# Batch 0's q through TensorE, low parts of w_spatial moved, and a new written order in a memory-attention and spatial-gate kernel

## The chip, the cores and the metric

One NeuronCore of a Trainium2 chip runs the whole program. Its engines work in parallel, each through its own queue in order: TensorE (PE; its weight loads are PEld), VectorE (DVE), ScalarE (ACT), GpSimd (POOL), and SyncE (SP), which issues all the loads and stores. The metric is the device time of one execution in microseconds. The kernel before was timed three times: median 435.25 us, from 434.84 to 436.11.

## The reference

Two stages over 8 batches, 8 heads, 576 positions, head size 64 and 32 memory slots. The first is an attention over memories that are weighted means of k and v:

```
a = softmax(phi over the 32 slots)                 # (b, h, s, m)
k_m, v_m = a^T k, a^T v                            # (b, h, m, d)
attn = softmax(q k_m^T / 8);  x = attn v_m         # heads side by side: (b, s, 512)
```

The second is a gated layer with a mixing over the positions:

```
h = relu(x @ w_in);  u, v = h[..., :512], h[..., 512:]
v_n = (v - mean(v)) / sqrt(var(v) + 1e-6)
v_s = w_spatial @ v_n + b_spatial[:, None]         # over the 576 positions
out = (u * v_s) @ w_out
```

w_in is 512 x 1024, w_spatial 576 x 576, w_out 512 x 512. w_in and w_out arrive as float64 and the other inputs as float32.

## The kernel before

Every large product is made from parts. A matrix is cut into a high part that TensorE takes at its fast rate and a low part, the rest (`hi`, `lo`; in names `h` and `l`), and three products, high by high, high by low and low by high, add up in PSUM. The low part is made in one of two ways by `low` (lines 152 to 163): VectorE subtracts the high part from the value in PSUM, or TensorE adds minus the high part to that PSUM tile (the matrix `minus`, line 157) and ScalarE copies the rest out. The set `ON_VECTOR` (line 50) says by name which way is taken, and in the same manner which engine does the additions and multiplications of the decoding.

w_in and w_out are decoded on the chip from the two 32-bit words of each float64 (`decode`, lines 177 to 223): VectorE takes the exponent (`power`) and the mantissa, ScalarE converts, and VectorE or GpSimd adds and multiplies. w_in comes in eight pieces of 128 rows and 512 columns; pairs of pieces are decoded together, E0 and E1 for the v half of w_in, L0 and L1 for the u half.

For each batch there are nine kinds of work, each a Python generator that yields between steps: P (softmax weights of phi), K (loads k and v, makes the memories: `kvm`, then the transposes `tk` and `tv`, then `kT` and `vT`), Q (loads q and transposes it into `qT`), S (scores `sc`, softmax `sm`, then `aT` and its parts `ah` and `al`), M (products `mp` of v_m with w_in, parts `mh` and `ml`), U (`pu`, the u half), V (`pv`, the v half with its normalization), G (`ps`, the mixing with w_spatial, times u, parts `gh` and `gl`), and O (`po`, the projection, and the store). Weights have their own kinds: D loads w_in, E and L decode it, X decodes w_out, W loads w_spatial, T transposes it (T0 to T3 by 128 columns, T4 the last 64; tiles `wt`, results `wth`, `wtl`, `ws1`, `ws2`), B sets the bias.

Nothing schedules this at run time. The string `START` (line 26) lists the steps of batch 0 and of all the weights, with the first steps of batches 1 and 2 (a prime is one batch ahead); `PLAN` (line 41) is the repeated list for batches 1 to 7. Each step issues its instructions at once, so these strings set the order in each engine's queue, that of SP's loads included. PSUM has four tiles of one bank (`bank`) and two of two banks (`banks`) that all the kinds share in turn: an instruction that writes a tile waits until the readers of its last use are done.

Batch 0's q is loaded in four transfers (lines 429 to 438), each of 32 partitions and runs of 32 floats, and VectorE transposes blocks of 32 by 32 (line 441).

Of the kernel before, what the change touches and what calls it, by code (L numbers as in the profile page):

```python
# [23 lines left out]


START = """
    D1 P W T3 P T3 B D0 T3 D0 T3 P*2 D1 T3 T2 L0 P E0 D1 T2*2 P T2 T3*2 P K P E0*2 L0 D1 P*2 K
    L0*2 E1 W P D0 L0 T2 P W D0 T1*2 E0 K T2 T1 E0 P W Q E1*2 L0 T1 E1 P L0 P E1 T1 E0*2 K T1 L1
    E0 Q K E1 P' L1 K L0 T2 L1 T1 E1 L1*2 K W E1 T4 K*2 L1 Q*3 K Q K'*2 P' K*2 P' T0 S P' S T0
    S*3 P' M1 P' S M1 T0 M1 P'*2 L1 P' M1 S P' S B M1 S L1 S P' T4*2 X1 T4*2 X0 T0 S M1 T0 M0 P'  # L30
    M1 P' S M0 K' T0 T4 M0 S M0 T0 T4 P' S M0 S*3 X0*2 S X0 P' S K' M0 X1 U0 X1*2 X0 U1 V1 M0 X0
    Q' V0 X1 X0 V1 X0 K'*2 V1 K' V0 X1*2 K' Q' U0 U1 X0 V3 U1 K' X1 U0 K' V1*2 U2 V2 V0 X1 V3*2
    V4 V1*2 X0 K'*2 V0 Q'*2 V0*3 V4 U3 U2 V2 Q' U3 X1 X0 Q' U2 V4 V3*2 U3 S' V2 S'*2 X1 S' V2 S'
    P'' X2 V2 X2 S' Q'' G0 X3 G1 M0' V3 V4 M1' V3 V2 V4*2 V2 P'' M1' X2 V4*2 K'' M0' G1 X2*2 M0'
    G0 P'' M1' G1 M1' P'' G0 P'' G1 G0 P'' M0' K'' G1 G3 X3 G0 S' G2 X2 P'' G1 G0 G3 X2 M1' G1
    X2 G0 M0' G2 M1' X3 G1 P'' G3 M0' P'' G2 G3 G0*2 G1 P'' G2 X2 M0' S' X3 G3 X3*2 X2 X3 O3 G2
    S' X3 O2 G2 G3 M1' G2 O1 X2 O0 X3*2 G3*2 G2 X3 G2 O3 S' P'' S' O1 S'*2 O3*2 P'' S' O1 O2 S'
    O0 S'*2 P'' O2 S'*2 P'' O1 G3 O2 P'' O0*2
"""

PLAN = """
    P'*4 K' U0 V1 V0 K' U0 V2 U0 K' U2 V0 V1 U1 V1 V0 V2 V1 V2 K' V0 V4 U1 V1 V3 Q' K' V0 P'' V1
    U1 K' U3 U2 V1 Q' V4 V2 V3 K' V2 V4 V3 K'*2 P''*4 U3 V4 K' S' U2 U3 V2 V3 V4 K'' S' V3 S'*2
    G0 V4 V3 G1 P'' S' M0'*2 Q'' P'' M1' G0 S' V2 S' M1' V4 G1 M1' V4 G0 V3 S' G1 Q G0 M1' M0'
    M1' P'' S' G1 G0 P'' M1' G2 S' G1 K'' G1 M0' S' G0 S' G1 G0*2 Q'' G3 G0 G2 S' G1 G3 G1 G2 G3
    G2 P'' S' G2*2 M1' G3*2 O3 G3 S'*2 O0 S' G2 G3 O1 O0 G3 P'' S' O0 S' O0 O1 O3 G3 Q'' O3 O4
    M0' G2 O3 O2 O1 V0' G2 O4 M0'*2 O1 O4 V0' Q'' O2 O4 O2*2
"""
# [9 lines left out]
def memory_attention_spatial_gate(  # L58
# [386 lines left out]
    def scores(b, _):  # L447
# [42 lines left out]
        state["a", b] = ah, al  # L490
        for r in range(2):
            for c in range(2):
                nc.vector.transpose(
                    aT[:, r].rearrange("p (i c x) -> p c i x", c=2, x=32)[:, c], sm[:, r, c]
                )
# [6 lines left out]
            yield
# [264 lines left out]
```

## Time and profile before

| | |
|---|---|
| median of 3 runs | 435.25 us |
| the profiled execution | 435.84 us |
| its span, first to last instruction | 434.1 us |
| TensorE busy | 400.4 us (92%) |
| VectorE busy | 294.9 us (68%) |
| ScalarE busy | 223.0 us (51%) |
| GpSimd busy | 74.0 us (17%) |
| mean granted TensorE clock | 0.971 |

The shares are means over the whole span, and the span has two unlike parts: the first 58 us, in which weights are loaded, decoded and transposed and the attention of batch 0 is made, and the rest. Line 634 (mixing) has 28% of the chain that ended last, line 674 (projection) 23%.

### The profile page before, as it was taken

The page shows a single profiled execution, that of the slowest core. Times are in us where ns is not written, and L with a number is a line of the kernel's source. Part 1 is how long each engine was busy: PE and PEld are TensorE (multiplying, and loading weights), DVE is VectorE, ACT ScalarE, POOL GpSimd, SP SyncE. Part 2 cuts the span into 40 slices and gives each one's busy share as a digit, 9 for nine tenths or more (in the row PEclk, how much of TensorE's full clock was granted, in tenths as well). Part 3 has the DMA queues.
Part 4 walks back from the last instruction along what each step waited for, and adds up shares of the span by engine and source line. Part 5 has one row for each costly group of instructions (what it writes and reads, how often), then busy time and mean ns, then how long its engine had stood idle before and what let it go on. Part 6 is the DMA issues. An engine that isn't in the chain of part 4 may idle for free.

```text
span 434.1 us, 9211 instructions
## 1 busy us (share of the span) xinstructions
PE 400.4 (92%) x3815; PEld 333.1 (77%) x3815; DVE 294.9 (68%) x546; ACT 223.0 (51%) x427; POOL 74.0 (17%) x148
## 2 busy tenths in 40 slices
PE   0436699999999999999999999999999999999996
PEld 0233297988889787988888887988798787988985
DVE  1599989995899338954898349954896358824420
ACT  1663578753854348343943368244833276337412
POOL 1007237240400032000400022002300030003000
PEclk9985689999999999999999999999999999999999
DMA  8999916807890169403980359214940300010003
GB/s 292 405 192 360 123 57 99 271 0 149 208 181 2 72 179 210 47 24 113 204 142 2 112 176 203 16 73 132 210 68 24 98 2 2 2 74 23 2 2 121
DMA packets 94543, 50.69 MB, mean 117 GB/s; under 512 B 75491, under 2 KB 79587, under 8 KB 94501
## 3 DMA queue, kind: packets, MB, share of 16 engines
q1 hardware_dynamic: 94500, 50.10, 47.5%
q8 instruction: 30, 0.49, 0.5%
q14 instruction: 13, 0.10, 0.1%
HBM read 40.65 MB, written 9.44 MB: 115 GB/s over the span
## 4 chain that ended last, share of the span: by engine, by line
PE 87%; DVE 6%; DMA 4%; ACT 1%; issue 1%; SPq 0%; DVEq 0%; ACTq 0%
PE ps L634 28%; PE po L674 23%; PE pv L547 13%; PE pu L596 12%; PE kvm L371 4%; PE mp L517 4%; DMA raw<-in_moe_w_in_dram 2%; DMA w_rem<-in_moe_w_spatial_dram 2%; PE sc L455 2%; DVE power L206 1%; DVE win_sb L214 1%; DVE win_sb L219 1%; DVE qT L441 1%; DVE half L317 0%; DVE g L645 0%
## 5 line engine op out<-in xcount | busy, mean ns | idle before, releaser
L634 PE MATMUL ps<-wth,vh 128*128 128x288 f32 x256 | 57.8, 307 | 0.1
L559 POOL TENSOR_SCALAR rs<-mv 128x1 f32<-128x1 f32 (+1 forms) x40 | 10.1, 253 | 262.7 <-DVE mv L556 238.0
L634 PE MATMUL ps<-wth,vl 128*128 128x288 f32 x256 | 54.6, 295 | 0.0
L634 PE MATMUL ps<-wtl,vh 128*128 128x288 f32 x256 | 54.5, 294 | 0.0
L674 PE MATMUL po<-wol,gh 128*128 128x512 f32 x128 | 50.8, 397 | 0.0
L674 PE MATMUL po<-woh,gh 128*128 128x512 f32 x128 | 50.6, 395 | 0.0
L674 PE MATMUL po<-woh,gl 128*128 128x512 f32 x128 | 50.2, 392 | 0.0
L680 ACT COPY o<-po 128x512 f32<-128x512 f32 x36 | 21.2, 588 | 55.8 <-PE po L674 53.5
L634 PEld LDWEIGHTS ps<-wth,vh 128*128 128x128 f32 x256 | 40.4, 188 | 10.9 <-issue 5.9
L554 DVE BATCH_NORM_STATS2 st<-vr 128x6 f32<-128x512 f32 (+1 forms) x40 | 27.3, 682 | 29.8 <-ACT vr L551 29.6
L656 ACT CAST gh<-g 128x512 fp32r<-128x512 f32 x32 | 19.1, 620 | 49.1 <-DVE g L645 49.1
L634 PEld LDWEIGHTS ps<-wtl,vh 128*128 128x128 f32 x256 | 41.2, 188 | 0.0
L634 PEld LDWEIGHTS ps<-wth,vl 128*128 128x128 f32 x256 | 41.0, 188 | 0.0
L605 ACT ACTIVATE u<-pu 128x576 f32<-128x576 f32 x32 | 20.2, 659 | 30.6 <-PE pu L596 30.2
L569 ACT ACTIVATE vr<-vr,sh,rs 128x512 f32<-128x512 f32 (+1 forms) x40 | 31.9, 817 | 5.4 <-POOL sh L564 5.4
L547 PE MATMUL pv<-mh,al 128*128 128x512 f32 (+1 forms) x80 | 31.6, 395 | 0.0
L547 PE MATMUL pv<-mh,ah 128*128 128x512 f32 (+1 forms) x80 | 31.6, 395 | 0.0
L547 PE MATMUL pv<-ml,ah 128*128 128x512 f32 (+1 forms) x80 | 31.6, 395 | 0.0
L658 DVE TENSOR_TENSOR grl<-g,grh 128x64 fp32r<-128x64 f32 x32 | 6.7, 213 | 36.3 <-ACT grh L656 36.3
L645 DVE TENSOR_TENSOR g<-u,ps 128x576 f32<-128x576 f32 x32 | 24.1, 752 | 9.7 <-PE ps L634 9.5
L596 PE MATMUL pu<-ah,mh 128*128 128x288 f32 x128 | 29.2, 309 | 0.0
L371 PE MATMUL kvm<-kv_sb,phi_sb 64*32 64x128 f32 x1152 | 23.3, 300 | 5.8 <-DMA kv_sb<-in_v_dram 5.0
(137 smaller groups left out, 876.9 us busy)
## 6 DMA issues: line engine op xcount, KB each, us to landing
kv_sb<-in_k_dram SPq DMA_DIRECT2D x8, 1152.0 KB, 7.7
kv_sb<-in_v_dram SPq DMA_DIRECT2D x8, 1152.0 KB, 10.3
q_sb<-in_q_dram SPq DMA_DIRECT2D x32, 288.0 KB, 7.0
out_dram<-o SPq DMA_DIRECT2D x32, 256.0 KB, 2.0
phi_sb<-in_phi_dram SPq DMA_DIRECT2D x8, 576.0 KB, 4.7
raw<-in_moe_w_in_dram SPq DMA_DIRECT2D x8, 512.0 KB, 9.5
raw_out<-in_moe_w_out_dram SPq DMA_DIRECT2D x4, 512.0 KB, 10.3
w_sb<-in_moe_w_spatial_dram SPq DMA_DIRECT2D x1, 1152.0 KB, 8.6
```

Of the source, the lines that this page charges most:

```text
L371: nc.tensor.matmul(kvm[r][32 * j : 32 * j + 32], phi_sb[halves[r], j, i, :], kv_sb[halves[r], j, :, i * D : (i + 1) * D], start=(i == 0), ...
L517: nc.tensor.matmul(mps[r][32 * j : 32 * j + 32, :], vT[D * r : D * r + D, 32 * j : 32 * j + 32], win_sb[D * r : D * r + D, j, cs], start=True,
L547: nc.tensor.matmul(pv, x[:, r, cs], m[:, r, DM:DFF], start=(n == 0), stop=(n == 5))
L554: nc.vector.bn_stats(st6, vr)
L569: nc.scalar.activation(vr, vr, AF.Identity, bias=sh, scale=rs)
L596: nc.tensor.matmul(pu[:, hf, 0:HALF], m[:, r, cs], a[:, r, hf * HALF : (hf + 1) * HALF], start=(n == 0), stop=(n == 5),)
L605: nc.scalar.activation(u[:, dt, :].rearrange("p (a s) -> p a s", a=2), pu[:, :, 0:HALF], AF.Relu)
L634: nc.tensor.matmul(ps[:, hf, 0:HALF], a, w[:, hf * HALF : (hf + 1) * HALF], start=(n == 0), stop=(n == len(ops) - 1),)
L645: nc.vector.tensor_tensor(g.rearrange("p (a s) -> p a s", a=2), u[:, dt, :].rearrange("p (a s) -> p a s", a=2), ps[:, :, 0:HALF], op=ALU.mult,
L656: nc.scalar.copy(hi, x)
L674: nc.tensor.matmul(po, a, w, start=(n == 0), stop=(n == 11))
L680: nc.scalar.copy(o, po)
```

## The change

There are four parts. In `low`, TensorE's way now takes tiles of fewer than 128 rows, and `transpose_spatial` passes a name for every low part, so that each can go either way. `queries` has a branch for batch 0: one load in the layout of k and v, TensorE transposes it into PSUM tiles `tq`, and ScalarE copies them into `qT`. The positions then stand in another order, and `scores` puts them back when it transposes `sm` into `aT`, in two transposes for each one of before. `START` and `PLAN` are rewritten, and `ON_VECTOR` with them: E1's addition and multiplication leave VectorE for ScalarE and GpSimd, L1's come to VectorE, L0's multiplication goes to GpSimd; of the low parts of w_spatial, three stay on VectorE (`wtl10`, `wtl1512`, `wtl40`) and seven are made by TensorE and ScalarE, where three were before.

```
 START = """
-    D1 P W T3 P T3 B D0 T3 D0 T3 P*2 D1 T3 T2 L0 P E0 D1 T2*2 P T2 T3*2 P K P E0*2 L0 D1 P*2 K
...
+    P*6 W D0 P*4 T1 P D1 B D1 E0 T2*2 D0 T2 D0 P*3 L0 T2 P T1 L0 T1 T2 L0 D0 L1 E0 T1 L0 T1 L1*2
...
 PLAN = """
-    P'*4 K' U0 V1 V0 K' U0 V2 U0 K' U2 V0 V1 U1 V1 V0 V2 V1 V2 K' V0 V4 U1 V1 V3 Q' K' V0 P'' V1
...
+    U0 P'*3 K' P' V1 V0 U0 K' U0 K' V2 U2 V0 V1*3 U1 V2 V0 V2 V0 V4 U1 V1 V0 V2 K' Q' P'' V1 U1
...
 ON_VECTOR = set(
-    es0 E0.add E0.mul E1.add E1.mul L0.add L0.mul ml000 wtl2 X0.add X1.add X1.mul X3.wol ml110
-    ml111 ml100 ml101 es2 es3 es4 es5 es6 es7
+    E0.add E0.mul L0.add L1.add L1.mul wtl10 wtl1512 wtl40 X0.add X1.add X1.mul X1.wol es1 ml110
+    ml111 ml100 ml101 es2 es3 es5 es6 es7
...
         if tensor:
-            tensor.matmul(x, minus, hi, start=False, stop=True, skip_group_check=True)
+            n = x.shape[0]
+            tensor.matmul(
+                x, minus[0:n, 0:n], hi, start=False, stop=True, skip_group_check=True
+            )
...
             if si < NI:
-                yield from low(f"wtl{si}" if cs.start == 0 else None, wtl[:, si, cs], part, hi)
+                yield from low(f"wtl{si}{cs.start}", wtl[:, si, cs], part, hi)
             else:
-                yield from low(None, ws2[0:SR, cs], part[0:SR], hi[0:SR])
+                yield from low(f"wtl{si}{cs.start}", ws2[0:SR, cs], part[0:SR], hi[0:SR])
...
     def queries(b, _):
+        if b == 0:
+            q_sb = one.tile([P, NJ, NX * D], F32, tag="q_sb", name="q_all")
+            nc.sync.dma_start(
+                q_sb, q[b].rearrange("(j r) (p i) d -> (r p) j (i d)", r=2, i=NX)
+            )
+            yield
+            qT = state["qT", b] = one.tile([P, H, HALF], F32, name="qT")
+            for j in range(NJ):
+                tq = bank(f"tq_{j}")
+                for n in range(4):
+                    cs = slice(n * P, (n + 1) * P)
+                    nc.tensor.transpose(tq[:, cs], q_sb[:, j, cs], ident)
+                yield
+                nc.scalar.copy(
+                    qT[:, 2 * j : 2 * j + 2, 0:256].rearrange("p r (i s) -> p r i s", s=64),
+                    tq.rearrange("p (i r s) -> p r i s", r=2, s=64),
+                )
+                yield
+            tq = bank("tq_4")
+
+            for j in range(NJ):
+                cs = slice(j * P, (j + 1) * P)
+                nc.tensor.transpose(tq[:, cs], q_sb[:, j, 7 * D :], ident)
+                nc.tensor.transpose(tq[0:D, cs], q_sb[:, j, 8 * D :], ident)
+            yield
+            for c in range(2):
+                rows = slice(D * c, D * c + D)
+                nc.scalar.copy(
+                    qT[rows, :, 256:],
+                    tq[rows].rearrange("p (h s) -> p h s", s=64)[:, :, 32 * c : 32 * c + 32],
+                )
+                yield
+            return
         q_sb = one.tile([P, H, NX, 32], F32, name="q_sb")
...
     def scores(b, _):
...
         for r in range(2):
             for c in range(2):
-                nc.vector.transpose(
-                    aT[:, r].rearrange("p (i c x) -> p c i x", c=2, x=32)[:, c], sm[:, r, c]
-                )
+                if b == 0:
+                    to = aT[:, r].rearrange("p (h x i) -> p i h x", x=32, i=NX)
+                    nc.vector.transpose(
+                        to[:, c:8:2], sm[:, r, c, 0:8].rearrange("p (i h) m -> p i h m", h=2)
+                    )
+                    nc.vector.transpose(to[:, 8, c], sm[:, r, c, 8])
+                else:
+                    nc.vector.transpose(
+                        aT[:, r].rearrange("p (i c x) -> p c i x", c=2, x=32)[:, c], sm[:, r, c]
+                    )
```

Three places show what the new strings move. The first is TensorE between the products of batch 0's memories and its scores; `tk` and `tv` are the transposes of the memories, `wt_4` and `wt_0` those of w_spatial, `tq` those of q. Before:

```order
L383 MATMUL kvm_0_1_185<-ones_88,es_171 32x2
L283 MATMUL wt_4_308<-ident_73,w_dup_163 128x128 x4
L283 MATMUL wt_4_308<-ident_73,w_rem_dup_164 128x64
L411 MATMUL tk_0_317<-ident_73,kmn_296 128x128 x2
L416 MATMUL tv_0_325<-ident_73,vmn_314 128x128
L283 MATMUL wt_0_338<-ident_73,w_sb_102 128x128 x4
L283 MATMUL wt_0_338<-ident_73,w_rem_103 128x64
L455 MATMUL sc_0_0_0_344<-qT_321,kT_333 32x288
```

Now:

```order
L387 MATMUL kvm_0_1_199<-ones_88,es_149 32x2
L287 MATMUL wt_4_283<-ident_73,w_dup_176 128x128 x4
L287 MATMUL wt_4_283<-ident_73,w_rem_dup_177 128x64
L443 MATMUL tq_0_299<-ident_73,q_all_182 128x128 x4
L415 MATMUL tk_0_310<-ident_73,kmn_296 128x128 x2
L420 MATMUL tv_0_318<-ident_73,vmn_307 128x128
L443 MATMUL tq_1_327<-ident_73,q_all_182 128x128 x4
L443 MATMUL tq_2_334<-ident_73,q_all_182 128x128 x4
L443 MATMUL tq_3_340<-ident_73,q_all_182 128x128 x4
L454 MATMUL tq_4_346<-ident_73,q_all_182 128x128
L455 MATMUL tq_4_346<-ident_73,q_all_182 64x128
L492 MATMUL sc_0_0_0_361<-qT_298,kT_320 32x288
```

The transposes `wt_0` have gone ahead of `kvm`, and five groups of transposes of q stand between the memories and the scores.

The second is ScalarE's queue from the casts of w_spatial's first transposes (`wth`, `wtl`) through the decoding of w_in (`power` and `raw`); the bracket names the engines and load queues whose signals the instruction waits for. Before:

```order
L204 ACTIVATE raw_121<-raw_121 128x1024 [waits DMAHW7_49,DMAHW6_49]
L294 CAST wth_93<-wt_2_130 128x64
L267 COPY w_rem_dup_164<-w_rem_103 64x64 [waits DMAHW3_49]
L294 CAST wth_93<-wt_1_176 128x512 [waits PE_49]
L201 ACTIVATE power_139<-power_139,rebias_81 128x1024
L204 ACTIVATE raw_99<-raw_99 128x1024 [waits DMAHW0_49]
L265 COPY w_dup_163<-w_sb_102 128x4x64
L160 CAST wtl_94<-wt_1_176 128x512 [waits PE_49]
L201 ACTIVATE power_161<-power_161,rebias_81 128x1024 [waits DVE_49]
L204 ACTIVATE raw_141<-raw_141 128x1024 [waits DMAHW3_49,DMAHW1_49]
L294 CAST wth_93<-wt_1_176 128x64
```

Now (136 is E0's power, 154 L0's, 162 L1's):

```order
L205 ACTIVATE power_154<-power_154,rebias_81 128x1024 [waits DVE_49]
L298 CAST wth_93<-wt_1_125 128x64 [waits DVE_49]
L205 ACTIVATE power_136<-power_136,rebias_81 128x1024
L208 ACTIVATE raw_116<-raw_116 128x1024 [waits DMAHW5_49,DMAHW0_49]
L205 ACTIVATE power_162<-power_162,rebias_81 128x1024
L208 ACTIVATE raw_132<-raw_132 128x1024 [waits DMAHW7_49,DMAHW6_49]
L269 COPY w_dup_176<-w_sb_108 128x4x64 [waits DMAHW1_49]
L271 COPY w_rem_dup_177<-w_rem_109 64x64 [waits DMAHW2_49]
L164 CAST wtl_94<-wt_2_138 128x64 [waits PE_49]
L269 COPY w_dup_176<-w_sb_108 128x4x64
L208 ACTIVATE raw_147<-raw_147 128x1024 [waits DMAHW2_49,DMAHW1_49]
```

The 64-column cast of `wt_1` stands early, behind a wait for VectorE, and the activations of three decodings follow it, with the last copy out of `wt_2` behind those.

The third is VectorE's queue at the scores of batch 0 (`sc` into `sm`, its maxima `rmx`, and `phi_sb` of batch 1 between). Before:

```order
L466 STREAM_TRANSPOSE sm_365<-sc_0_0_0_344 128x288
L466 STREAM_TRANSPOSE sm_365<-sc_0_0_1_345 128x288
L466 STREAM_TRANSPOSE sm_365<-sc_0_1_0_346 128x288
L466 STREAM_TRANSPOSE sm_365<-sc_0_1_1_347 128x288
L321 TENSOR_TENSOR mx_330<-mx_330,phi_sb_86 128x128
L472 TENSOR_REDUCE rmx_386<-sm_365 128x36
L337 TENSOR_REDUCE cm_391<-mt_1_384 128x2
L475 TENSOR_TENSOR sm_365<-sm_365,rmx_386 128x1152
L345 TENSOR_TENSOR phi_sb_86<-phi_sb_86,mb_1_397 128x1152
L480 TENSOR_REDUCE rsum_405<-sm_365 128x36
```

Now:

```order
L503 STREAM_TRANSPOSE sm_383<-sc_0_0_1_362 128x288
L325 TENSOR_TENSOR mx_355<-mx_355,phi_sb_86 128x128
L503 STREAM_TRANSPOSE sm_383<-sc_0_1_0_363 128x288
L503 STREAM_TRANSPOSE sm_383<-sc_0_1_1_364 128x288
L341 TENSOR_REDUCE cm_409<-mt_1_391 128x2
L509 TENSOR_REDUCE rmx_413<-sm_383 128x36
L210 SCALAR_TENSOR_TENSOR power_314<-raw_188,power_314 128x1024
L512 TENSOR_TENSOR sm_383<-sm_383,rmx_413 128x1152
L349 TENSOR_TENSOR phi_sb_86<-phi_sb_86,mb_1_424 128x1152
L517 TENSOR_REDUCE rsum_456<-sm_383 128x36
L519 TENSOR_SCALAR rsum_456<-rsum_456 128x36
L520 RECIPROCAL rsum_456<-rsum_456 128x36
```

An instruction of E1's decoding (`power_314`) has come between the maxima and the subtraction, and the batch 1 maxima `mx` stand between the transposes.

## Rows read from the trace of the kernel before

**Rows 1.** The page's 40 slices: busy tenths of TensorE and VectorE.

```profile
PE   0436699999999999999999999999999999999996
...
DVE  1599989995899338954898349954896358824420
```

**Rows 2.** Chain that ended last: start us, us, engine, result, line.

```profile
10.96 9.32 DMA raw<-in_moe_w_in_dram
...
37.50 2.67 DVE qT L441 x4
...
43.87 2.32 PE mp L517 x16
...
53.51 3.67 PE kvm L371 x129
...
57.93 1.59 PE pu L596 x12
...
59.52 2.80 PE pv L547 x12
...
430.45 0.59 ACT o L680
```

**Rows 3.** Timeline of SP: start us, us, queue, line, transfer.

```profile
13.83 16.12 SPq L432 DMA_DIRECT2D q_sb<-in_q_dram  x4
...
30.13 2.12 SPq L326 DMA_DIRECT2D phi_sb<-in_phi_dram  x1
```

**Rows 4.** Windows: stretch, length, busy per engine, PEclk, DMA share, GB/s.

```profile
20.00:21.00 1.00, 0.00 (x0) 0.00 (x0) 0.63 (x2) 1.00 (x3) 0.00 (x0) 1.00 1.05 393
...
31.00:32.00 1.00, 0.00 (x0) 0.00 (x0) 1.00 (x2) 0.49 (x1) 0.00 (x0) 0.50 1.51 165
...
48.00:50.00 2.00, 0.08 (x1) 0.08 (x1) 2.00 (x3) 1.81 (x4) 0.00 (x0) 1.00 1.23 145
```

**Rows 5.** Timeline, loads and ScalarE: start us, us, engine, line, work.

```profile
23.41 2.39 PE L371 MATMUL kvm<-kv_sb,phi_sb 64*32 64x128 f32 x80 [5.01 <-DMA kv_sb<-in_v_dram]
...
33.51 1.15 ACT L204 ACTIVATE raw<-raw 128x1024 f32<-128x1024 uint32 x1
...
37.47 0.59 ACT L294 CAST wth<-wt 128x512 fp32r<-128x512 f32 x1 [0.82 <-PE wt L283]
...
52.15 0.21 ACT L294 CAST ws<-wt 128x64 fp32r<-128x64 f32 x1 [0.75 <-DVE ws L162]
```

**Rows 6.** Timeline of TensorE: transposes and scores at both clock levels.

```profile
32.89 1.09 PE L283 MATMUL wt<-ident,w_dup 128*128 128x128 f32 x4 [5.25 <-DVE wtl L162]
...
35.38 0.69 PE L411 MATMUL tk<-ident,kmn 128*128 128x128 f32 x2
...
65.14 0.38 PE L411 MATMUL tk<-ident,kmn 128*128 128x128 f32 x2
...
71.53 1.20 PE L455 MATMUL sc<-qT,kT 64*32 64x288 f32 x32
```

**Rows 7.** Timeline: GpSimd and VectorE working at the same time.

```profile
29.66 1.21 DVE L206 SCALAR_TENSOR_TENSOR power<-raw,power 128x1024 int32<-128x1024 int32 x1
...
34.80 3.84 POOL L212 TENSOR_TENSOR win_sb<-win_sb,raw 128x512 f32<-128x512 f32 x2 [32.35 <-ACT raw L204]
...
35.18 2.32 DVE L206 SCALAR_TENSOR_TENSOR power<-raw,power 128x1024 int32<-128x1024 int32 x1
...
80.82 1.32 POOL L212 TENSOR_TENSOR raw_out<-raw_out 128x512 f32<-128x512 f32 x1 [5.02 <-ACT raw_out L204]
...
81.12 0.76 DVE L645 TENSOR_TENSOR g<-u,ps 128x576 f32<-128x576 f32 x1
```

**Rows 8.** Timeline of VectorE: scores of batch 0 and later.

```profile
43.35 1.56 DVE L466 STREAM_TRANSPOSE sm<-sc 128x288 f32<-128x288 f32 x4
...
48.11 1.35 DVE L345 TENSOR_TENSOR phi_sb<-phi_sb,mb 128x1152 f32<-128x1152 f32 x1
...
94.13 1.28 DVE L658 TENSOR_TENSOR gl<-g,gh 128x512 fp32r<-128x512 f32 x2
```

More of the change, by code (lines that the diff above doesn't have):

```diff
@@ L26 @@
 START = """
-    D1 P W T3 P T3 B D0 T3 D0 T3 P*2 D1 T3 T2 L0 P E0 D1 T2*2 P T2 T3*2 P K P E0*2 L0 D1 P*2 K
[L28 to L38, printed above, removed]
+    P*6 W D0 P*4 T1 P D1 B D1 E0 T2*2 D0 T2 D0 P*3 L0 T2 P T1 L0 T1 T2 L0 D0 L1 E0 T1 L0 T1 L1*2
@@ new lines @@
+    K E0*2 L0 T1 T2 L1 E0 K W*2 E0 L0 Q E0 T2 W L1 D1 T0 W D1 K E0 T1 K L1 T4 L0 L1 K L1 K Q K
+    L0 K*2 T0 E1 T4 E1 T4 K*3 Q P' T4 Q K' Q*6 P'*2 Q*2 S K' E1 S P' S T0 P' T4 S P' M0 E1 T4 S
+    E1 P'*2 S T4 M0 X0 M0 E1 T0*3 P' M0 T3 S M0 S P' T3 E1 M0 E1 P' M0 T3 M1 S*2 X1 T0 M1*2 T3
+    P' M1 K' S T3 P' S*2 M1 S P'*2 Q' S T3 M1 K' S Q' U1 M1 T3 S K' U0 S K' X0 K'*2 S K' X1 K'
+    X0*3 X1 X0 X1*2 V0 V1 X1 U1 V1 U0 V3 X0 B K' V0 X0 U1 X1*2 V1 U2 X1 U0 X1 V0 U3 X1 X0 P'' X0
+    V1 Q'*2 U2 V3 V0 V2 K' Q' V1 X2 V1 V0 V3 V1 X0 U3 U2 V0*2 Q' V2*2 U3 V4*2 G0 P'' V3 V4 G1 S'
@@ L39 @@
+    V3 V2*2 S' V4 S' V3 S' G1 S' V2*2 V4 X3 V4 V3 V4 G0 M1' M0'*2 X2 G1 P'' V4 G0 M1' M0' P'' G1
+    M0' M1' X2 X3 M1' X3 X2 K'' X2*2 P'' M0' G1 G0*2 M1' P'' M1' X2 G3 X3 G1 G2 P'' M0' X2 G3 X3
+    G0 S' P'' G0 X3 G2 S' G3 G1*3 X2 M0' M1' G2 S' G3 X3*3 G2 X2 G0*2 P'' G3 G2 G3 Q'' P'' X2 X3
+    G2 S' O1 O0 G3 G2 O3 P'' S'*3 X3 G3 O2 O1 O0 S' G2 O1 K'' O3 O1 O2 S'*2 O0 S' P'' O3 G2 O0
+    S'*3 O3 G3 O2 P'' O2 P''*2
 """
 PLAN = """
-    P'*4 K' U0 V1 V0 K' U0 V2 U0 K' U2 V0 V1 U1 V1 V0 V2 V1 V2 K' V0 V4 U1 V1 V3 Q' K' V0 P'' V1
@@ L43 @@
[L43 to L47, printed above, removed]
+    U0 P'*3 K' P' V1 V0 U0 K' U0 K' V2 U2 V0 V1*3 U1 V2 V0 V2 V0 V4 U1 V1 V0 V2 K' Q' P'' V1 U1
@@ L48 @@
+    V3 U3 Q' U2 V1 V4*2 K' V2 P'' K'*2 P'' V3 P'' K' P'' V3 V4 K' K'' U3 K' S' U2 U3 V2 V4 S' V3
+    S' V3 S'*2 G0 V4 G1 P'' M0' Q'' P'' M1' M0' S' V3 V2 S' M1'*2 G0 V4 G1 G0 V3 S' G1 V4 G0 P''
+    M1' S' M0' Q G1 G0 M1' G0 S' G1 S' M1' K'' P'' G0 S' Q'' G1 G0*2 M0' G2 G3 P'' G2 S' G3 G1*3
+    G2 G3 G2*3 M1' G3 O3 G2 S' G3 S'*2 O0 G3 S' O1 G3 O0 S' G3 P'' M0' S' O3 O0 G2 O0 G3 O1 O3
+    M0' O3 O4 G2 Q'' O2 M0' O1 O4 O1 V0' O2 O4*2 Q'' O2 V0' O2
 """
```

## The prediction

> **What bounds the kernel now.** I read the page's slices first. TensorE stands at 9 from the sixth slice (54 us) on, VectorE at 9 or 8 from the third slice to the ninth [rows 1]. So the run is a start-up in which TensorE mostly waits, and then seven and a half batches in which it does not. The chain of waits says the same [rows 2]: a load of w_in ends it until 20.28 us (10.96 + 9.32), VectorE carries it past 40 us, with the four transposes of q (2.67 us) among its links, and from 53.51 us it runs on TensorE: the products kvm of batch 1, then the first pu at 57.93, the first pv at 59.52, and from there to the last copy at 430.45. Whatever the start-up saves or loses before the first pv is therefore carried to the end, as long as VectorE and ScalarE keep up behind it. The profiled run took 435.84 us, 1.7 more than its span of 434.1, and 0.59 more than the median 435.25; I sum against the profiled run and then take off 0.59.
>
> My mark is "all of the start-up done and pv begins". Before: 59.52; the after order has also done tk and tv of batch 1 by then (two transposes 0.38 at the high clock level [rows 6], with overlap some 0.35 for both), so a tie would be a first pv at 59.9.
>
> **The loads.** The four q loads move runs of 128 bytes; while they run, the core gets 165 GB/s against 393 for the loads ahead of them [rows 4], and SP sits in their issue for 16.12 us [rows 3], so the phi load of batch 1 is not issued before 30.13. One load with runs of 2304 bytes replaces them; I price it as those of k, same shape: 1.18 MB at 0.393 MB/us, 3.0 us. Before, VectorE met q with no idle time, so the load itself was hidden; what the faster load buys is room, not time by itself. The order of the loads gives landing times: before, the piece that landed at 20.28 had 6.24 MB up to and with it. After, the last piece of L1 has 5.06 MB: 3.0 us less, 17.3. v is unchanged in its sum, and lands as before at 23.4 [rows 5]. q: 26.4. E1's last piece: 29.1.
>
> **ScalarE gets a wait.** The 64-column cast of wt_1 now stands behind VectorE's low part of the same tile. That such a cast waits is seen for ws: 0.75 us on VectorE [rows 5]. VectorE reaches that low part only after the power of L1 (17.3), two field extractions and itself, some 2.0 us: 19.3. Behind the cast ScalarE has queued four activations of 1024 columns (1.15 each [rows 5], some 1.05 from start to start), two copies and the 64-column wtl of wt_2: 4.9 us more, 24.4. That last copy frees the PSUM tile for the transposes wt_0 (1.09 + 0.3), and only behind these stand the products kvm of batch 0: they start at 25.8 instead of 23.4. The new order loses 2.4 us here. It could lose nothing, if ScalarE did not wait, or 3.5, if L1 lands a microsecond later.
>
> **q through TensorE.** kvm and the sums take what they took, less one lo matmul that has moved: 3.6 us, to 29.4. den, kmn (both halves), tk and tv as before, about 2.4 us, to 31.8; tq_0 and wt_4 run in this gap and cost nothing while it stands. Then TensorE and ScalarE alternate: tq_1 to tq_3 with four transposes each (1.09 us at the low level [rows 6]; at the high level about half, since tk's pair took 0.38 instead of 0.69), each released by a copy of 512 columns (0.59 [rows 5]), then eight transposes and two half copies. With kT, vT and two copies ahead this is 7.0 us at the low level, 4.7 at the high one: the last copy at 38.8 or 36.5. The scores took 1.20 us for 32 at the high level [rows 6], so the first half is there 0.6 us later, 1.2 at the low level. VectorE's first sm transpose, at 43.35 before [rows 8], comes at 37.1 to 40.0. The level: the granted clock was 0.50 (1.2 GHz) at 31 to 32 us, when TensorE had been idle, and 1.00 (2.4 GHz) at 48 to 50, after a run of mp products of 2.32 us [rows 2, 4]. In the new order TensorE works from 24.4 on with small gaps; I take 38.3, a little to the high side. VectorE is free by then: the four transposes of q (2.67) and one multiplication of L0 (1.14) have left it, and it is done with E1's extraction near 35.
>
> **From there to pv.** Before, 43.35 to 59.52: 16.2 us. After, this stretch is longer, because the last w_in half to be decoded, E1, comes here and through ScalarE and GpSimd. After the last q copy (1.2 us before the sm mark) ScalarE does three activations of E1, 3.3 us: mark + 2.1. GpSimd then does two additions and two multiplications of 512 columns. Two took 3.84 us beside VectorE, one took 1.32 alone [rows 7]: 5.3 to 7.7 us for four. I take 7.0, near the pair in the same place: mark + 9.1. mp for E1, 2.32 us [rows 2]: 11.4. mh 0.59, the lo matmul 0.8: 12.8. kvm of batch 1, 3.67 [rows 2], with two lo matmuls and a ScalarE queue between its halves, 0.5: 17.0. pu 1.59: 18.6; the kmn of batch 1 behind it lets tk start 0.3 late, tk and tv 0.4: pv at mark + 19.3. Bounds: 17.9 with the lower GpSimd price, 20.7 with the higher one and all at the low level. VectorE's own chain in this stretch gains one E1 instruction (1.21 [rows 7]), the sums es1 (which about cancel with low parts that left it) and one collision with GpSimd, and ends ah and al of the first half at about mark + 16, so it is covered by TensorE's. The four small lo matmuls and copies of w_spatial stand in gaps and cost nothing of their own.
>
> So pv begins at 38.3 + 19.3 = 57.6, 2.3 us before the tie, between 55.0 and 60.7.
>
> **After pv.** VectorE enters this stretch with the decoding of X0 still to do, some 4 us of work that before stood ahead of den, and had 2.5 us of idle to spend. The second half of the first projection needs the gl that ended at 95.41 [rows 8], and TensorE came to it half a microsecond later. I charge 0.4 us, from 0 to 2. PLAN is nearly the same sequence; TensorE has no idle time in those batches to give or lose: 0, give or take 0.5.
>
> Sum: 435.84 - 2.3 + 0.4 = 433.9 for a run like the profiled one, 433.4 for the median.
>
> **A rule to weigh.** When GpSimd added for L1, VectorE's L206 took 2.32 us instead of 1.21; but a product with a PSUM operand, inside a GpSimd addition at 80.82, took 0.76, its usual length [rows 7]. The Trainium skill, "SBUF — State Buffer", section "SBUF: two separate sides", says that the pair of ports the two engines share is an exclusive lock held for a whole instruction, taken by VectorE when it has two SBUF inputs. By this sentence up to four VectorE instructions of the stretch to pv can lose one GpSimd instruction each, 1.32 us; were all of it on the path, the time would be some 4 us higher. The rows bear the lock out; that it falls on the path is the third rival.
>
> **Rivals.**
> 1. VectorE is the bound to 95 us, and what TensorE gains it waits away before the first projection's second half. For it: VectorE at 9 in the slices from 76 to 98 us, and only 0.5 us of slack there. Against: VectorE's work before that point falls by about 4.5 us (q 2.67, L0 1.14, low parts of w_spatial 0.5, one ml 0.65, less 0.5 for more and smaller aT transposes). Time: the gain shrinks to 0.3, median 435.0.
> 2. The high clock holds through the start-up, and GpSimd runs near its lower price: mark 37.2, pv at mark + 18.4 = 55.6, gain 4.3, less 0.6 behind: 431.5. For it: TensorE's longer work from 24.4 on. Against: gaps of about a microsecond while ScalarE copies.
> 3. Slower: GpSimd's four E1 instructions, each behind a locked VectorE instruction, hold up mp of E1, and kvm of batch 1 and pu behind it in TensorE's queue. Price: each at 1.92 + 0.6, mark + 12.2 for the last, pv at mark + 22.4; with the mark at 39.0 that is 61.4, 1.5 us past the tie, plus 0.6 behind: 437.3. It decides once E1's last product comes later than mark + 11.
>
> **How the numbers follow.** Chances: the forecast 0.38, rival 1 0.26, rival 2 0.15, rival 3 0.21. What a measurement can tell is 0.3%, 1.3 us, so faster means under 433.9 and slower over 436.6. The forecast lies 0.5 under that line and goes into same in a third of its cases; rival 1 is same in most; rival 3 slower in three of four. Faster: 0.26 + 0.15 + 0.08 = 0.49; same 0.34; slower 0.17. The forecast's own range is 432.0 to 435.0; eight in ten reach from 430.8 (rival 2 with its bound) to 436.9.
>
> **What would show it.** In the profile after: the 64-column cast of wt_1 on ScalarE waiting for VectorE until about 19 us; kvm of batch 0 starting near 26; the first sm near 38 (over 40: the low level held); GpSimd's four E1 instructions ending near mark + 9; the first pv near 57.6; TensorE without idle time over 0.5 us between there and the first projection. The prediction is wrong if sm comes later than 41, if pv comes after 60, or if TensorE shows new waits on VectorE between 60 and 100 us.

## The result and the profile after

The kernel after takes 431.08 us (median of 4 runs, 430.96 to 431.32) where the kernel before, in the same job, takes 435.11 (4 runs, 434.84 to 436.11). The ratio is 0.9906, 95% interval 0.9881 to 0.9932: 0.9% faster, with the interval clear of 1. The profiled run of after took 431.01 us with a span of 429.2, against 435.84 and 434.1. So the two traces differ by 4.9 us, 0.9 more than the medians do (4.0), since the profiled run of before was 0.7 above its median.

The page's slices of after, in tenths: TensorE and the granted clock.

```profile
PE   3176799999999999999999999999999999999996
...
PEclk9999699999999999999999999999999999999999
```

TensorE is at 9 from the sixth slice on, as in [rows 1]. Its third slice has risen from 3 to 7, and only one slice, the fifth, shows a lower clock. The chain that ended last in after (start us, us, engine, result, line):

```profile
8.90 7.46 DMA raw<-in_moe_w_in_dram
...
31.70 1.95 ACT qT L445 x4
...
38.60 1.65 DVE power L210
40.25 2.36 DVE sm L512
...
43.91 0.38 ACT wth L298
44.34 0.79 PE wt L159
45.13 2.02 PE mp L561 x16
...
48.57 2.31 PE kvm L375 x80
...
54.89 2.80 PE pv L591 x12
```

Read it against [rows 2]. The load of w_in ends at 16.36 instead of 20.28. VectorE's four transposes of q are gone, and ScalarE's copies of q stand there. The first pv comes at 54.89 instead of 59.52. By then the new order has done tk and tv, so the tie was 59.9 and the gain is 5.0 us, the difference of the spans to 0.1: behind the first pv nothing more than that was lost or won.

The timeline of after, from four engines (start us, us, engine, line, work, in brackets the idle time before and who ended it):

```profile
16.45 0.69 DVE L187 TENSOR_SCALAR power<-raw 128x1024 int32<-128x1024 int32 x1 [0.96 <-DMA raw<-in_moe_w_in_dram]
...
18.38 0.21 ACT L298 CAST wth<-wt 128x64 fp32r<-128x64 f32 x1 [2.57 <-DVE wtl L166]
...
24.64 1.74 PE L375 MATMUL kvm<-kv_sb,phi_sb 64*32 64x128 f32 x56
...
30.51 0.60 PE L443 MATMUL tq<-ident,q_all 128*128 128x128 f32 x4
...
31.53 2.12 ACT L445 COPY qT<-tq 128x512 f32<-128x512 f32 x4
31.58 1.09 PE L443 MATMUL tq<-ident,q_all 128*128 128x128 f32 x8 [0.47 <-ACT kT L424]
...
32.65 0.68 DVE L193 TENSOR_SCALAR win_sb<-raw 128x1024 int32<-128x1024 int32 x1
...
33.59 0.76 ACT L459 COPY qT<-tq 64x256 f32<-64x256 f32 x2
...
35.19 0.48 DVE L503 STREAM_TRANSPOSE sm<-sc 128x288 f32<-128x288 f32 x1 [0.20 <-PE sc L492]
...
37.88 3.51 POOL L216 TENSOR_TENSOR win_sb<-win_sb,raw 128x512 f32<-128x512 f32 x2 [5.71 <-ACT raw L208]
...
38.52 1.73 DVE L210 SCALAR_TENSOR_TENSOR power<-raw,power 128x1024 int32<-128x1024 int32 x1
40.17 2.44 DVE L512 TENSOR_TENSOR sm<-sm,rmx 128x1152 f32<-128x1152 f32 x1
...
41.36 3.62 POOL L226 TENSOR_TENSOR win_sb<-win_sb,power 128x512 f32<-128x512 f32 x2
...
43.84 1.35 DVE L517 TENSOR_REDUCE rsum<-sm 128x36 f32<-128x1152 f32 x1
...
44.34 0.79 PE L159 MATMUL wt<-wth,minus 128*128 128x512 f32 x1 [3.29 <-ACT wth L298]
...
45.06 1.41 POOL L310 TENSOR_TENSOR ws<-b_sb,ws 1x576 fp32r<-1x576 f32 x1
...
45.23 1.28 DVE L519 TENSOR_SCALAR rsum<-rsum 128x36 f32<-128x36 f32 x1
```

The reader is to see three things. ScalarE's 64-column cast does wait for VectorE, until 18.38. The transposes of q (L443) and the copies (L445) run side by side, not in turn. And VectorE's L210, L512 and L519, which run beside GpSimd's work, are long (1.73, 2.44 and 1.28 us); the reduction L517, beside it too, is not. The windows of after (stretch, length, busy of PE, PEld, DVE, ACT, POOL, clock, DMA share, GB/s) give the rate of the loads and the clock:

```profile
12.00:14.00 2.00, 0.80 (x1) 0.29 (x1) 1.30 (x2) 1.12 (x3) 1.84 (x3) 1.00 1.03 420
...
30.00:32.00 2.00, 1.45 (x11) 1.02 (x11) 2.00 (x2) 2.00 (x7) 2.00 (x1) 1.00 1.02 374
...
42.00:44.00 2.00, 0.00 (x0) 0.00 (x0) 2.00 (x3) 1.35 (x2) 2.00 (x2) 0.98 0.99 146
44.00:46.00 2.00, 1.66 (x17) 0.51 (x17) 1.97 (x2) 1.94 (x4) 1.92 (x2) 0.50 1.13 146
```

The clock is at 1.00 (2.4 GHz) while q is transposed, where it was 0.50 (1.2 GHz) at the same time before [rows 4]. It falls only near 44 us, in a stretch from 41.0 to 44.3 in which TensorE is idle.

### The profile page after: what moved, and what is told of

It reads as the page before. It is cut to its first block, busy times and chain, and to the rows that moved or that the text cites. A ratio compares the mean times of both kernels' runs of the same rounds, so it can differ in the third digit from the quotient of the medians.

```text
span 429.2 us, 9278 instructions
## 1 busy us (share of the span) xinstructions
PE 399.7 (93%) x3844; PEld 335.9 (78%) x3844; DVE 292.5 (68%) x536; ACT 228.3 (53%) x438; POOL 81.7 (19%) x154
## 4 chain that ended last, share of the span: by engine, by line
PE 89%; DVE 4%; DMA 3%; ACT 2%; issue 1%; SPq 0%; ACTq 0%; DVEq 0%
PE ps L678 29%; PE po L718 23%; PE pv L591 14%; PE pu L640 12%; PE kvm L375 4%; PE mp L561 4%; PE sc L492 2%; DMA raw<-in_moe_w_in_dram 2%; DMA w_rem<-in_moe_w_spatial_dram 2%; DVE win_sb L218 1%; DVE power L210 1%; DVE sm L512 1%; ACT raw L208 1%; ACT qT L445 0%; DVE g L689 0%
## 5 line engine op out<-in xcount | busy, mean ns | idle before, releaser
L603 POOL TENSOR_SCALAR rs<-mv 128x1 f32<-128x1 f32 (+1 forms) x40 | 11.6, 291 | 236.1 <-DVE mv L600 232.1
L591 PE MATMUL pv<-mh,ah 128*128 128x512 f32 (+1 forms) x80 | 32.9, 411 | 0.0
L595 ACT ACTIVATE vr<-pv 128x512 f32<-128x512 f32 (+1 forms) x40 | 23.8, 595 | 14.6 <-PE pv L591 14.6
L718 PEld LDWEIGHTS po<-woh,gl 128*128 128x128 f32 x128 | 24.0, 188 | 5.7
L718 PEld LDWEIGHTS po<-woh,gh 128*128 128x128 f32 x128 | 24.0, 188 | 5.2
```

The source lines that it names most:

```text
L591: nc.tensor.matmul(pv, x[:, r, cs], m[:, r, DM:DFF], start=(n == 0), stop=(n == 5))
L595: nc.scalar.activation(vr, pv, AF.Relu)
L718: nc.tensor.matmul(po, a, w, start=(n == 0), stop=(n == 11))
```

## The experiments

All runs in one table: the first sm transpose on VectorE, the first pv in the chain, the span, and what is left of the span after that pv; then the median with lowest and highest, and the ratio to the kernel before run beside it, with its interval. The runs stand in four groups, and the kernel before had medians of 435.11 (beside after), 435.48 (x1, x2, x3, x5), 434.86 (x4, x6, x7, x8) and 435.09 (x9 to x12): a difference of a few tenths between kernels of two groups is not clear of that spread.

| kernel | first sm | first pv | span | rest | median us | ratio |
|---|---|---|---|---|---|---|
| before | 43.35 | 59.52 | 434.1 | 374.6 | 435.11 (434.84 to 436.11) | |
| after | 35.19 | 54.89 | 429.2 | 374.3 | 431.08 (430.96 to 431.32) | 0.9906 [0.9881, 0.9932] |
| x1_old_q | 41.31 | 60.79 | 435.0 | 374.2 | 436.56 (435.54 to 437.07) | 1.0024 [1.0011, 1.0037] |
| x2_q_alone | 41.76 | 57.63 | 432.2 | 374.6 | 433.79 (432.95 to 435.31) | 0.9968 [0.9953, 0.9984] |
| x3_lo_before | 34.16 | 54.15 | 428.6 | 374.4 | 430.90 (430.38 to 431.41) | 0.9896 [0.9877, 0.9915] |
| x5_wtl1_tensor | 33.58 | 53.54 | 427.9 | 374.4 | 429.56 (429.17 to 430.14) | 0.9867 [0.9847, 0.9886] |
| x4_E1_vector | 36.18 | 55.51 | 429.9 | 374.4 | 431.65 (431.63 to 431.70) | 0.9921 [0.9903, 0.9940] |
| x6_hold_clock | 35.23 | 55.16 | 429.5 | 374.3 | 431.32 (431.22 to 431.50) | 0.9914 [0.9897, 0.9931] |
| x7_plan_before | 35.22 | 55.97 | 430.4 | 374.4 | 431.58 (431.17 to 432.22) | 0.9921 [0.9902, 0.9939] |
| x8_combined | 34.29 | 54.34 | 428.6 | 374.3 | 430.39 (429.85 to 430.40) | 0.9889 [0.9870, 0.9908] |
| x9_bias_early | 33.79 | 54.23 | 428.6 | 374.4 | 429.78 (429.25 to 430.34) | 0.9873 [0.9852, 0.9894] |
| x10_all | 33.49 | 53.47 | 427.8 | 374.3 | 429.31 (428.72 to 429.59) | 0.9864 [0.9846, 0.9882] |
| x11_phi_first | 33.46 | 52.80 | 427.1 | 374.3 | 428.99 (428.81 to 429.91) | 0.9863 [0.9844, 0.9882] |
| x12_one_tile | 41.82 | 62.08 | 436.4 | 374.3 | 436.60 (436.48 to 438.14) | 1.0038 [1.0024, 1.0052] |

The column "rest" is the first finding: in fourteen kernels it is 374.2 to 374.6, and the two at 374.6 still have tk and tv, 0.33 us, behind that pv. The span of a profiled run is the time of its first pv and a constant.

**x1_old_q**: after, with batch 0's q on its old path.

```
     def queries(b, _):
-        if b == 0:
+        if False:
...
-                if b == 0:
+                if False:
                     to = aT[:, r].rearrange("p (h x i) -> p i h x", x=32, i=NX)
```

> The changed kernel with batch 0's q loaded and transposed as before (four loads of 128-byte runs, four VectorE transposes), order and sets as changed. My theory: VectorE's relief counts, and the slow load stands ahead of E1's last pieces, whose extraction VectorE then waits for: 2.7 to 5 us slower than the changed kernel's 431.1, so 433.8 to 436. Rival, the new order alone made the gain: 430.6 to 431.6.

Slower than expected, and 0.24% slower than before. Two pieces of its chain:

```profile
25.38 9.43 DMA q_sb<-in_q_dram
...
36.04 0.78 DVE qT L478
```

The new order asks for the scores near 34 us, and the four old loads of q end at 34.8. VectorE then still has to transpose it, and the first sm comes 6.1 us later than in after.

**x2_q_alone**: before, with the new q path and six more Q steps in START (`Q*3` becomes `Q*9`).

> The kernel before with only the q part: one load, TensorE transposes, ScalarE copies, the two-piece aT transposes; the order as before, with six more Q steps where four of them stood. My theory: VectorE, which sets the pace there, loses 2.67 us of transposes and the later loads come sooner, so 1.5 to 2.7 us faster than before's 435.1: 432.4 to 433.6. Rival, the gain is the order's: 434.6 to 435.6. Rival, q is only better with its steps placed for it, since eight TensorE and ScalarE steps in one block wait on each other: slower, 436 or more.

433.79, 1.7 us below the 435.48 of before beside it: 0.2 above the expected stretch. So the path alone gives 1.7, the new order and sets alone cost 1.1, and all together give 4.0 (435.11 to 431.08). Neither part explains the gain by itself. The order brings the scores forward only if q is there. Its timeline also shows q's transposes at the low level:

```profile
35.65 2.77 PE L439 MATMUL tq<-ident,q_all 128*128 128x128 f32 x12
...
39.35 0.74 ACT L455 COPY qT<-tq 64x256 f32<-64x256 f32 x2 [0.32 <-PE tq L451]
```

From tq_1 to the last copy it is 35.65 to 40.09, 4.4 us, against 30.51 to 34.35, 3.8 us, in after. There transposes and copies overlap too, with the clock at 0.50 from 34 to 38 us and at 0.91 from 38 to 40. The difference of 0.6 is no clean price of the clock, since the stretch in after holds a wait of 0.47 us for kT's copy, which this one does not.

**x3_lo_before**: after, with the low parts of w_spatial as they were, five of them back on VectorE.

```
-    E0.add E0.mul L0.add L1.add L1.mul wtl10 wtl1512 wtl40
+    E0.add E0.mul L0.add L1.add L1.mul wtl1512 wtl40 wtl20 wtl0512 wtl2512 wtl3512 wtl4512
```

> The changed kernel with the low parts of w_spatial on the engines that made them before (three by TensorE, seven by VectorE). My theory: they stand in gaps; VectorE has 0.5 us more: 431.1 to 431.7. Rival, their move carries a good part of the gain: 432.5 or more.

430.90, the same as after within the intervals. It mixes two things: `wtl10` goes to TensorE, so that the 64-column cast no longer waits until 18.4, and five more subtractions go to VectorE. The next run has the first edit, with one more small part off VectorE and none put back, and is 1.3 us faster than this one (0.6 in the first pv of the two traces), so the five cost about that at most, unless the small part was better left on VectorE.

**x5_wtl1_tensor**: after, with both low parts of w_spatial's tile 1 off VectorE.

```
-    E0.add E0.mul L0.add L1.add L1.mul wtl10 wtl1512 wtl40
+    E0.add E0.mul L0.add L1.add L1.mul wtl40
```

> The changed kernel with wt_1's two low parts made by TensorE and ScalarE, so that ScalarE's 64-column cast of wt_1 does not wait for VectorE (2.57 us idle in the trace of the changed kernel). My theory, the wait is on the path through kvm and the decoding: 1.5 to 2.5 us faster than 431.1, so 428.6 to 429.6. Rival, what follows is bound by the landing of q and E1 and the wait is covered: 430.6 to 431.3.

429.56, inside the expectation; its highest run is below the lowest of after. The timeline shows the cast and kvm of batch 0:

```profile
15.09 0.58 ACT L163 CAST wtl<-wt 128x512 fp32r<-128x512 f32 x1 [0.76 <-PE wt L158]
...
16.74 0.19 ACT L297 CAST wth<-wt 128x64 fp32r<-128x64 f32 x1
...
23.01 3.85 PE L374 MATMUL kvm<-kv_sb,phi_sb 64*32 64x128 f32 x144
```

The cast stands 1.6 us earlier and without a wait, kvm starts 1.6 us earlier, the first sm 1.6, the first pv 1.35. So of what the cast gains nearly all reaches the first pv. It gains less than the 2.57 us of idle time, since ScalarE now makes the low part of 512 columns itself (0.58 us, after 0.76 of waiting for TensorE).

**x4_E1_vector**: after, with `E1.add E1.mul` in ON_VECTOR.

> The kernel after, with E1's addition and multiplication back on VectorE (two instructions of 1024 columns, about 1.15 us each) in place of GpSimd's four, which took 7.1 us from 37.9 to 45.0. Theory (the lock is a tie): VectorE gains back what it lost beside GpSimd, 0.5 on the exponent merge, 1.1 on the subtraction of the maxima and 1.1 on the small sum, 2.7 us, and pays 2.3 for the two instructions; E1 is ready near 44.4 instead of 45.0. pv begins 0.4 to 0.6 earlier: 430.6 us, within 430.0 and 431.4. Rival (GpSimd's price alone holds TensorE up): mp of E1 goes at 43.0 and everything behind it 2 us earlier: 429.0. Third (VectorE's chain is the only bound): it stands 0.4 us shorter, 430.7, but with low parts later, up to 431.5.

431.65, a miss by 1 us on the wrong side. From its timeline:

```profile
32.31 1.74 POOL L309 TENSOR_TENSOR ws<-b_sb,ws 1x576 fp32r<-1x576 f32 x1
...
32.71 1.90 DVE L192 TENSOR_SCALAR win_sb<-raw 128x1024 int32<-128x1024 int32 x1
...
40.63 1.35 DVE L511 TENSOR_TENSOR sm<-sm,rmx 128x1152 f32<-128x1152 f32 x1
...
46.94 0.18 DVE L518 TENSOR_SCALAR rsum<-rsum 128x36 f32<-128x36 f32 x1
```

The collisions beside E1's work are gone, as expected (1.35 instead of 2.44, 0.18 instead of 1.28). But GpSimd, with no E1 work, now does the small bias addition at 32.3 instead of 45.1, and VectorE's extraction beside it takes 1.90 instead of 0.68. The first sm comes 1.0 us late.

**x6_hold_clock**: after, with T3's transposes four times.

```
-        for ti in range(NI + 1):
+        for ti in [*range(NI + 1)] * (4 if si == 3 else 1):
```

> The kernel after, with the five transposes of w_spatial's tile 3 issued four times in place (same result), so that TensorE works through most of the 41.0 to 44.3 us in which it was idle before the clock fell to 0.50 until 51. Theory (TensorE's chain and VectorE's chain from the scores to pv end together): mp of E1, 2.02 us at the low level against 1.16 at the high one, and the products behind it gain 1.5 us, but den, kmn and al keep pv where it was to within 0.5: 430.6 to 431.1 us. Rival (the low level of 44 to 51 us is on the path in full): pv 1.3 to 1.5 us earlier, 429.7. The granted clock between 44 and 50 tells whether the repetition held it; if it stays at 0.50 nothing changes, 431.1, and the question stays open.

431.32. The profiled execution alone decides nothing, as the last sentence foresaw. In its timeline and windows:

```profile
44.59 0.79 PE L159 MATMUL wt<-wth,minus 128*128 128x512 f32 x1 [1.16 <-ACT wth L298]
```

```profile
44.00:46.00 2.00, 1.42 (x9) 0.51 (x17) 1.97 (x3) 2.00 (x5) 1.92 (x3) 0.61 1.19 151
```

The repetition fills TensorE until 43.4, and the clock falls near 44.4 instead of 44.0. The other executions decide it. The low stretch of about 7 us makes a mean clock of 0.992 over the run; three of the six executions have 0.998, 1.000 and 0.999, which leaves room for some 2 us at the low level at most (an estimate from the means). They took 431.40, 431.36 and 431.50 us, and the three with 0.992 took 431.22 to 431.28. With the clock up, this kernel is no faster: the theory holds to some tenths, and the rival's 429.7 is out.

**x7_plan_before**: after, with PLAN of the kernel before.

> The kernel after with the repeated list of batches 1 to 7 as it was in the kernel before. Theory (all of the gain lies ahead of the first pv, and the two lists differ only in small exchanges): 431.1 us, within 0.4. Rival (the new list carries a part of the gain): 432.0 or more.

431.58, between the two expectations (431.5 and 432.0). Its rest is 374.4. What it loses in the profiled run, it loses ahead of the first pv, where its instructions are those of after: there the clock came back later, and the second half of kvm took 1.85 instead of 0.99 us. The list carries no gain that these runs can show.

**x8_combined**: x5, with E1 on VectorE, ahead of phi, with T3's cast ahead of the exponential of the scores, and with phi's exponential behind the casts `mh`.

```
-    P' M0 T3 S M0 S P' T3 E1 M0 E1 P' M0 T3 M1 S*2 X1 T0 M1*2 T3 P' M1
+    P' M0 T3 S M0 T3 S E1*2 P' M0*2 T3 M1 S*2 X1 T0 M1*2 P' T3 P' M1
```

> The kernel after with three edits: both low parts of w_spatial's tile 1 on TensorE (as in the run that gave 429.56), E1's addition and multiplication on VectorE ahead of the subtraction for batch 1's phi, and the cast of w_spatial's tile 3 issued ahead of ScalarE's exponential of batch 0's scores, behind which TensorE waited 3.3 us for it. Theory: E1 is ready at 41.7 instead of 43.3, mp of E1 begins there, and VectorE's chain, 0.7 us shorter, sets the first pv near 52.2 to 52.8: 428.3 us, within 427.7 and 428.9. Rival (VectorE's chain through den and al bounds in any case and gains nothing): 429.6 as without the two further edits. On the other side: the low parts now ahead on ScalarE delay phi's exponential and with it kvm of batch 1: 430.2.

430.39, a miss, with the bias addition of x4 again (timeline):

```profile
30.42 1.75 POOL L298 TENSOR_TENSOR ws<-b_sb,ws 1x576 fp32r<-1x576 f32 x1
...
30.82 1.91 DVE L181 TENSOR_SCALAR win_sb<-raw 128x1024 int32<-128x1024 int32 x1
```

The first sm comes 0.7 us later than in x5.

**x9_bias_early**: x5, with the last step B moved from the end of START's list to the place ahead of `K E0*2`.

```
-    ... L1*2 K E0*2 ... V3 X0 B K' V0
+    ... L1*2 B K E0*2 ... V3 X0 K' V0
```

> The kernel with both low parts of w_spatial's tile 1 on TensorE (429.56 before), and GpSimd's one small addition of the bias (1 by 576, 1.41 us, at 43.4) issued ahead of the loads' decoding, near 15 us. Lock theory: VectorE's small sum, 1.29 us beside that addition, takes 0.18 again and its chain to al is 1.1 us shorter. TensorE's chain (mp of E1 released by GpSimd's own E1 work at 43.4) is not, so pv gains 0 to 0.3 us: 429.3 us. Rival (VectorE's chain alone set pv): 1.1 less, 428.5. No lock: the sum still takes 1.3 and the time is 429.6.

```profile
14.95 1.74 POOL L298 TENSOR_TENSOR ws<-b_sb,ws 1x576 fp32r<-1x576 f32 x1
...
43.86 0.18 DVE L507 TENSOR_SCALAR rsum<-rsum 128x36 f32<-128x36 f32 x1
...
52.27 0.22 DVE L385 TENSOR_SCALAR den<-kvm 128x1 f32<-128x1 f32 x2 [1.35 <-PE kvm L375]
```

One small GpSimd instruction moved, and VectorE's small sum falls from 1.29 to 0.18 us: the lock, alone. The time, 429.78, is that of x5 within their spreads, also where no lock would have put it (429.6), so that it is the instruction and not the time that tells. VectorE waits the gain away: 1.35 us for kvm ahead of den, where x5 shows 0.34. TensorE's chain was the later one there.

**x10_all** and **x11_phi_first**: x8 with B early; x11 has phi's exponential ahead of the casts (`E1*2 P' M0 P' M0 T3 M1`, the rest as in after).

> The combined kernel (430.39) with the bias addition issued early as well. There, with no E1 work ahead of it on GpSimd, the addition had come at 30.4 and VectorE's extraction beside it took 1.91 us instead of 0.68, so the scores' first transpose came 0.8 late. Lock theory: extraction back to 0.68, first sm at 33.6, pv 0.8 us earlier or, if TensorE's gap ahead of mp then leaves the clock at 1.00, 1.5: 429.2 us, within 428.4 and 429.6. Rival (phi's exponential, now behind mh, is what bounds): 430.4.

> The same as the kernel with all edits and the early bias addition, but phi's exponential of batch 1 stays right behind that of the scores, ahead of the casts of the products. VectorE then finds phi ready where in the combined kernel it waited 0.56 us, and kvm's inputs are there earlier; the cast mh of E1's products is not later as long as they end after 44.6. Theory (VectorE's chain is the bound there): 0.5 us below the kernel with all edits, 428.7. Rival (the casts are on the path): 0.3 to 0.6 above it, 429.6.

429.31 and 428.99, both near their theory's number and both below x8; the runs don't tell them from each other. Either is faster than before, and its highest run lies below the lowest of after, in another group. In the timeline of x10:

```profile
45.35 1.37 PE L363 MATMUL kvm<-kv_sb,phi_sb 64*32 64x128 f32 x80 [0.57 <-ACT phi_sb L344]
...
49.27 0.27 PE L375 MATMUL kvm<-ones,es 64*32 64x2 f32 x16 [0.77 <-DVE es L313]
...
52.48 0.58 PE L403 MATMUL tk<-ident,kmn 128*128 128x128 f32 x2 [0.56 <-ACT kmn L390]
```

There kvm of batch 1 runs at the high level, 1.37 us for the 80 that take 2.38 in after, and TensorE then waits for VectorE's sums and for ScalarE's kmn. That shows, in a kernel with E1 on VectorE, what x6 found from its times: TensorE's chain and VectorE's end together there, and most of what one gains alone it waits away.

**x12_one_tile**: after, with q's five groups through one PSUM tile.

```
+            tq = bank("tq_0")
             for j in range(NJ):
-                tq = bank(f"tq_{j}")
...
-            tq = bank("tq_4")
```

> The kernel after, with the five groups of q's transposes going through one PSUM tile instead of a new one each, so that each waits for the copy of the one before: the alternation that the prediction assumed. Theory (they overlap in the kernel after, and that, with the earlier landing, is why the scores came 3.1 us sooner than predicted): the last copy of q comes at 36.4 to 37.8 instead of 34.35, and the time rises by 2.0 to 3.4 us, to 433.1 to 434.5. Rival (the overlap is worth little, and the clock level and the landing did it): under 432.

436.60, two microseconds beyond the theory's range, on the theory's side. Timeline and windows:

```profile
32.35 1.11 PE L443 MATMUL tq<-ident,q_all 128*128 128x128 f32 x4 [1.56 <-ACT qT L445]
33.50 0.58 ACT L445 COPY qT<-tq 128x512 f32<-128x512 f32 x1 [1.20 <-PE tq L443]
34.14 1.12 PE L443 MATMUL tq<-ident,q_all 128*128 128x128 f32 x4 [0.68 <-ACT qT L445]
...
39.73 0.76 ACT L458 COPY qT<-tq 64x256 f32<-64x256 f32 x2 [2.06 <-PE tq L454]
...
41.82 0.48 DVE L502 STREAM_TRANSPOSE sm<-sc 128x288 f32<-128x288 f32 x1 [7.04 <-PE sc L491]
```

```profile
32.00:34.00 2.00, 1.11 (x4) 0.71 (x4) 2.00 (x4) 0.80 (x2) 0.00 (x0) 0.58 1.06 410
34.00:36.00 2.00, 1.19 (x5) 0.79 (x6) 0.75 (x2) 0.67 (x2) 0.00 (x0) 0.50 1.06 393
```

Taking turns, TensorE waits 1.56 us for the first copy and 0.68 for each one after, and the clock falls to 0.50: four transposes take 1.11 instead of 0.60. The last copy ends at 40.49 instead of 34.35, 6.1 us later. The profiled execution is the slowest of the eight, 438.14, 1.5 above the median, and the traces don't show where a typical one is shorter; the medians are 5.5 us apart. The expectation had the turns and not the clock that they cost.

## Why the prediction was right, and where its sizes were not

The direction and the mechanism held: the start-up is shorter, and the rest stays. The time lies 2.3 us below the forecast of 433.4. That is outside the forecast's own range, 432.0 to 435.0, and inside the wide one, 430.8 to 436.9. The nearest number is rival 2's, 431.5, but not by its terms: sm came 2.0 us before rival 2's mark, the stretch from sm to pv was 1.3 longer, and nothing was paid behind pv. That the two agree to 0.4 us is in part luck.

- *The loads.* 17.3 predicted, 16.4 measured: 3.9 us earlier than before, where I wrote 3.0. I priced at 393 GB/s; from 12 to 14 us it was 420. That is not the reason, since at 420 the 1.18 MB less would have saved 2.8 us. Summed over the windows (an estimate), the core had moved some 7.0 MB when the piece of before landed at 20.28, and 5.4 MB at 16.36 in after: 1.6 MB less, not 1.18. Which loads make the other 0.4 MB stays open.
- *ScalarE's wait.* Predicted until 19.3, measured 18.38; behind it kvm at 25.8 and 24.64, so that it came 1.2 us later than before and not 2.4. Both moved with the landing. In x5, without the wait, kvm starts 1.6 us earlier and the first pv 1.35.
- *q through TensorE.* This step failed in its size: "Then TensorE and ScalarE alternate". I put the first sm at 38.3, bounds 37.1 to 40.0; it came at 35.19, outside. Of the 3.1 us, 1.3 were there when tq_1 began (30.51 instead of 31.8), from the landing and from the products being a little shorter. Another 1.5 are the stretch to the last copy, 3.84 us where the mark of 38.3 holds 5.3, and 0.4 the step from there to sm. Each group has its own PSUM tile, so the transposes stand beside the copies, and the sum over both engines was the wrong sum: at the high level it gave 4.7, 0.9 too much. The other 0.6 is my choice of a mark above the high level's, where the clock was at 1.00 all through. x12 shows turns between the engines, and with them the low level: its last copy is 6.1 us later, part of which may be its slow execution's. Rival 2 had the high clock level but not its reason: the gaps that stood against it in the prediction are in x12 and not in after.
- *From sm to pv.* 19.3 predicted, 19.7 measured. GpSimd's four E1 instructions took 7.1 us (3.51 and 3.62 for each pair) against 7.0, and ended at mark + 9.8 against 9.1. The third rival's lock was real, 0.5 on L210 and 1.1 each on L512 and L519 over their usual lengths, but GpSimd did not reach its point of decision, mark + 11. What I had not seen is a second path to the same place. The chain that ended last goes through L210 and L512, both lengthened, then the exponential and the cast of w_spatial's tile 3 on ScalarE, for which TensorE waits 3.29 us, and that tile's low part ends at 45.13. GpSimd's last E1 product ended at 44.98. So the two paths to mp of E1 are a tie, and my price for GpSimd's gave the right time for both.
- *After pv.* I charged 0.4 and it cost nothing: the rest is the same constant in all fourteen kernels. Rival 1, VectorE waiting the gain away, did not happen.
- *The low parts.* The four new lo matmuls on TensorE cost nothing that shows. x3 beside x5 says that on VectorE five such parts cost up to 1.3 us (0.6 by the two traces), which I had not counted as a gain.

The rule of the Trainium skill that I weighed ("SBUF — State Buffer", section "SBUF: two separate sides") agrees with the runs where VectorE has two SBUF inputs: L512 takes 2.44 us beside GpSimd's E1 work and 1.35 in x4 without it. I had told only one of the two conditions that the section gives for VectorE; the other is a perf mode that takes two ports. Which mode an instruction ran in, no row shows, so the runs can't tell whether L519 and the extraction, with one tensor input each, fell under it. That L519 is held up, x9 shows: it moves one GpSimd instruction and takes 1.1 us off it. My "some 4 us" for four instructions at 1.32 was a slip; the product is 5.3.

What stays open: whether the low clock from 44 to 51 us costs anything in the kernel after itself, whose four executions all show it (mean clock 0.988 to 0.992). In x6, which has T3's transposes repeated and is otherwise the same, it costs nothing. In x8, with E1 on VectorE, the one execution with a mean clock of 1.000 took 429.85 and the other four 430.26 to 430.40. The small moves in ON_VECTOR that came along (es0, es1, es4, ml000 and the wol parts) were not tried alone.

## What to carry to other kernels

Look for the one event after which the rest of the run is a constant, here the first pv, and read every edit as what it does to that event's time. Where two engines pass tiles to each other through several buffers, price the stretch by the slower engine, not by the sum of both; and where one buffer makes them take turns, see whether the clock stays up in the gaps, as it did not in x12. When work leaves an engine, look at what stands behind it in that engine's queue: it will run earlier, and may collide there with something on the path.
